# A fixed plan of scans per round, and row tiles loaded in the order in which the pairs change

## The chip, the cores and the metric

The kernel runs on one core of one Trainium2 chip. The metric is the device time of one execution in microseconds. Work on the core is done by TensorE (PE in the profile; PEld is its weight load), VectorE (DVE), ScalarE (ACT), GpSimd (POOL) and the DMA engines; SyncE (SP) issues most of the DMAs and computes nothing.

## What is computed

The input `x` has 2048 rows of 512 numbers, all float32. One half is softmax attention with 32 heads of 16 numbers each, the other a Fourier mixing of the same rows; a gate mixes the two.

```
g = sigmoid((x * gate_w).sum(-1, keepdims=True))
qkv = (x @ wqkv).reshape(B, S, 3, 32, 16)            # q, k, v
p = softmax(einsum("bhqd,bhkd->bhqk", q, k) * 16 ** -0.5, axis=-1)
a = einsum("bhqk,bhkd->bhqd", p, v).reshape(B, S, 512) @ wo
b = dft_seq_re @ (x @ dft_hid_re.T) - dft_seq_im @ (x @ dft_hid_im.T)
return g * a + (1 - g) * b
```

The weights are drawn large, so the softmax needs the row maximum taken off before the exponential.

## The kernel before

A **prologue** projects `x` to queries, keys and values, writes queries and keys to DRAM (`q_d`, `k_d`, each number as a high and a low part), and makes the operands of the Fourier half. Beside it run the first 320 **scans**. Then comes the **loop** `for m in range(MACROS)` of 256 rounds, and a short end.

The heads are handled in 16 **pairs** of two. For a pair two things are done, one after the other:

- **Scan** (`scan`, L624 and L626): the scores of a block of 128 queries against 512 keys are made on PE and reduced to their maximum by DVE (`mx<-s`). A pair takes 64 scans, each of two matmuls and two reductions (one for each head). When the last scan of a pair is done, `shift` (L179 to L182) turns the maxima into rows that are stored in `m_d`; its five parts stand in the list `late` and are given out among the tokens of the next two rounds.
- **Use** (`score`, L593 and L581; `pv`, L603): the scores are made again, transposed and with the maximum taken off inside the matmul, ACT takes their exponential, and PE multiplies by the values into the bank `pvb`. A pair takes 32 steps, that is 16 rounds; the first 8 rounds handle the first 1024 queries, the last 8 the others.

A **round** m holds two steps of use (8 scores and exponentials), some scans (before: 0 to 4), 6, 7 or 9 pairs of matmuls of the Fourier half and later of the output projection (`fill`, L840), and at its end the 16 value matmuls of the two steps before. The order of the matmuls in a round is written out by hand in a table `ORDERS`, by the numbers of scans and of fills; "c0 e1 s0" is a scan of head 0, a score of head 1, a fill of half 0.

Every 8 rounds (m = 8, 16, 24, ...) `pvb` is complete. `quotients` copies it on DVE (`ob`, L633), and POOL issues four small DMAs that gather the sums (`lc<-ob`, L636). At the head of round m + 2 DVE takes their reciprocal (`invert`, L643); it stands in DVE's queue ahead of all reductions of that round. POOL then spreads it and scales (rounds m + 4 and m + 6).

Scan and use of a pair each need its **row tiles** `qs` and `ks` (1.5 MB together) from DRAM, in two of six slots, so three pairs of tiles are held at a time: one in use, one being scanned, one loaded ahead. `load_scan` issues 8 DMAs on SP (L124); `load_use` issues the same 8 and then 6 small ones (ones, L138, and maxima from `m_d`, L140). SP takes its instructions in the order of the program; among them are the blocks of the Fourier matrices (`craw`, L208), stores (`y_d`, `bs_d`, `m_d`), and from time to time other loads. A slot falls free at the last matmul that reads it: for a pair in use at the end of a round 16p - 1, for a scanned one wherever its 64th scan stands.

Before, `prefetch(m)`, called at the head of each round, chooses what to load next when a slot pair is free: the next pair to scan or the next pair to use, by a guess of when the scan will end (`ends < 26`) and a rule that a pair to use is not loaded before the eighth step of the pair ahead. Scans are asked for at an even pace of 704/226 = 3.12 a round (`pace_`); a pair's first scan may be given only five rounds after its load (`scan_from`). Where the tiles are not there, a round gets fewer scans or none, and the next rounds get up to four until the plan is caught up with.

Of the kernel before, what the change touches and what calls it, by code (L numbers as in the profile page):

```python
# [23 lines left out]
NP = H // 2  # L24
# [7 lines left out]
PERIODS = 2 * NB  # L32
SCANS = 64
TOTAL = SCANS * NP
FRONT = 5 * SCANS
# [4 lines left out]
STEPS = NP * PERIODS  # L40
MACROS = STEPS // 2
OUTM = 234
SCAN_MACROS = 226
ENDS = {3: ("z0", "z1"), 8: ("z0", "z1"), 9: ("b3", "b4"), 10: ("b0", "b1"), 11: ("b2", "pv")}
ORDERS = {
# [12 lines left out]
def build(tc, x, xT, wqkv, wo, wrT, wiT, cr, ci, gate, out):  # L58
    nc = tc.nc
    with ExitStack() as ctx:  # L60
# [36 lines left out]
        def free_slots():  # L97
            return [i for i in range(6) if owner[i] is None]
# [10 lines left out]
        def release(who):  # L109
            for i in range(6):  # L110
                if owner[i] == who:
                    owner[i] = None

        def row_loads(p, queue, keys, who=None):

            qs, ks = (stacked([P, S], F32R, name, who) for name in ("qs", "ks"))
            loads = []
            for j in range(2):
                b, r = 64 * j, slice(DH * ((2 * p + j) % 8), DH * ((2 * p + j) % 8) + DH)
                loads += [(ks[b:b + 32, :], keys[p // 4][r, 0:1, :].to_broadcast([DH, 2, S])),  # L120
                          (qs[b:b + 32, :], q_d[p // 4][r, :, :].rearrange("e n s -> (e n) s")),
                          (ks[b + 32:b + 48, :], keys[p // 4][r, 1, :]),
                          (qs[b + 32:b + 48, :], q_d[p // 4][r, 0, :])]
            return (qs, ks), [lambda dst=dst, src=src: queue.dma_start(dst.bitcast(F32), src) for dst, src in loads]  # L124

        def load_scan(p, who=None):
            scanned[p], loads = row_loads(p, nc.sync, k_d, who)
            for load in loads:
                load()

        def load_use(p, who=None):
            used[p], loads = row_loads(p, nc.sync, k_d, who)
            for load in loads:
                load()
            qs, ks = used[p]
            for j in range(2):
                b = 64 * j + 48
                nc.sync.dma_start(ks[b:b + 2, :].bitcast(F32), ones_d)  # L138
                for n in range(2):
                    nc.sync.dma_start(qs[b + n:b + n + 1, :].bitcast(F32),  # L140
                                      m_d[p][n:n + 1, :, j].rearrange("n g b k -> n b g k"))
# [61 lines left out]
        def load_unit(pool, tag, bufs):  # L203
            if units:
                ph, t, u = units.pop(0)
                raw = pool.tile([P, D], F32, tag=tag, name="craw", bufs=bufs)
                raws_c.append(raw.rearrange("p (c q) -> p c q", q=P))
                nc.sync.dma_start(raws_c[-1], (cr, ci)[ph][t, :, u * CS:(u + 1) * CS, :])  # L208
# [12 lines left out]
        with ExitStack() as px:  # L221
# [101 lines left out]
            if True:  # L323
# [175 lines left out]
                def to_rhs(i):  # L499
                    def use(t, tx, ty):  # L500
                        ab = ep.tile([P, 512], F32, tag="eh", name="ab", bufs=3)
                        nc.gpsimd.tensor_add(ab, tx, ty)
                        after(7, nc.sync.dma_start, ab_d[i][t], ab)
                    return use
# [5 lines left out]
                use = to_rhs(1)  # L510
# [12 lines left out]
        with ExitStack() as pa:  # L523
# [23 lines left out]
            class Banks:  # L547

                slot, late, gap, load, group = 230.0, 434.0, 106.0, 200.0, 854.0
# [62 lines left out]
            scans, late = [FRONT, FRONT], []  # L612
# [93 lines left out]
            def output_rows(c):  # L706

                for f in range(ND - 1):
                    for i in range(2):
                        a = oc[c, f, i] = block((0, 18)[c % 2] + 2 * f + i)  # L710
                        src = o_d[f][i][c // 2, c % 2].rearrange("p (j r) s -> r (p j) s", j=2)
                        nc.sync.dma_start(a.bitcast(F32), src[0:DH])
# [10 lines left out]
            def load_y(c):  # L723
                y4 = stacked([P, 4, D], F32, "y4", ("y", c))
                nc.sync.dma_start(y4, y_d[c])
                for t in range(4 * c, 4 * c + 4):
                    ys[t] = y4[:, t % 4, :]
# [137 lines left out]
            def renew(s):  # L865
                ah[s], al[s] = block(2 * s), block(2 * s + 1)
                for i, v in enumerate((ah[s], al[s])):
                    nc.sync.dma_start(v.bitcast(F32), bs_d[s][i])
# [3 lines left out]
            def part_b(step):  # L872

                s, i = divmod(step, NB)
                for s, i in ((2 * s, i), (2 * s + 1, i - 4)):
                    if s < NB:
                        part_of_b(s, i)
# [22 lines left out]
            def order(nc_, ns):  # L900
                if (nc_, ns) in ORDERS:
                    return ORDERS[nc_, ns].split()
                base = ORDERS[(4, 7) if ns in (6, 7) else (0, 9)].split()
                for kind, have, want in (("c", 4 if ns < 9 else 0, nc_), ("s", 7 if ns < 9 else 9, ns)):
                    for j in range(2):
                        for _ in range(have - want):
                            base.remove(f"{kind}{j}")
                return base
# [3 lines left out]
            last = next_slot[0]  # L912
            for n, who in enumerate((("use", 0), ("use", 0), ("scan", FRONT // SCANS), ("scan", FRONT // SCANS))):
                owner[(last - 4 + n) % 6] = who
            use_loaded, scan_loaded = [0], [FRONT // SCANS]
            pace_ = (TOTAL - FRONT) / SCAN_MACROS
            scan_from = [0]

            def prefetch(m):

                p, i = divmod(2 * m, PERIODS)
                n = min(scans)
                while len(free_slots()) >= 2:
                    want_use = use_loaded[0] < NP - 1 and use_loaded[0] <= p and (
                        use_loaded[0] + 2) * SCANS <= n - 16 * bool(late)
                    want_scan = scan_loaded[0] < NP - 1 and scan_loaded[0] * SCANS <= n
                    ends = i + 2 * ((scan_loaded[0] + 1) * SCANS - n) / pace_
                    if want_scan and (not want_use or ends < 26):
                        scan_loaded[0] += 1
                        load_scan(scan_loaded[0], ("scan", scan_loaded[0]))  # L930
                        scan_from[0] = m + 5
                    elif want_use and i >= 8:
                        use_loaded[0] += 1
                        load_use(use_loaded[0], ("use", use_loaded[0]))
                    else:
                        return

            for m in range(MACROS):
                for step in (2 * m, 2 * m + 1):
                    part_b(step)  # L940
                for f in staged.pop(m, ()):
                    f()
                if m == 0:
                    for _ in range(2):
                        load_unit(ap, "craw", 2)
                if 2 * m % PERIODS == 0 and m:
                    release(("use", 2 * m // PERIODS - 1))
                prefetch(m)
                for ph, s in freed:
                    if ph == 0:  # L950
                        renew(s)
                    else:
                        if s == 2:
                            output_rows(0)
                        if s == 11:
                            output_rows(1)
                        if s in (5, 7, 9, 10, 11, 12):
                            next(operands, None)
                freed.clear()
                if m >= OUTM:  # L960
                    for _ in range(2):
                        next(operands, None)
                if m == OUTM - 2:
                    for c in range(2):
                        load_y(c)
                if 2 * m == (NP - 1) * PERIODS:
                    for c in (2, 3):
                        load_y(c)
                n = min(scans)
                want = min(TOTAL, FRONT + int(pace_ * (m + 1)))  # L970
                ready = min(TOTAL, (scan_loaded[0] + (m >= scan_from[0])) * SCANS)
                count_ = max(0, min(4, want - n, ready - n))
                for k, token in enumerate(order(count_, sizes[m])):
                    {"e": score, "c": scan, "s": fill}[token[0]](int(token[1]))
                    if late and k in (6, 13, 20):
                        late.pop(0)()
                for step in ((2 * m - 2, 2 * m - 1) if m else ()):
                    pv(step)
# [86 lines left out]
```

## Time and profile before

| | us |
|---|---|
| median of 3 runs | 1866.27 (1864.71 to 1867.63) |
| profiled execution, its own time | 1860.47 |
| its span | 1858.6 |
| PE busy | 1787.0 (96%) |
| DVE busy | 1334.2 (72%) |
| ACT busy | 1331.1 (72%) |
| POOL busy | 752.1 (40%) |

The profile shows one execution. The loop begins at about 365 us (the first score of L593) and ends near 1842 us (its last value matmuls); the rest is the prologue and the end. A round is seen most easily by its 16 value matmuls, which the view of the chain that ended last merges into one row, `PE pvb L603 x16`: the distance from one such row to the next is the length of a round. The columns of that view are the start in us, the length in us, and what ran.

### The profile page before, as it was taken

What the parts mean: (1) busy time and instruction counts of PE and PEld (TensorE: products, weight loads), DVE (VectorE), ACT (ScalarE), POOL (GpSimd) and SP (SyncE); (2) the same over time, 40 slices, a digit from 0 to 9 for tenths busy, and PEclk for the clock granted to TensorE, in tenths of its full rate; (3) what the DMA queues carried; (4) which work ended last, traced back from release to release, by engine and by line L of the source; (5) the groups of instructions that cost most, each with busy time, mean ns of one, the idle gap of its engine ahead of it and who ended that gap; (6) DMA issues with size and microseconds to landing.
All of it is one profiled execution on the core that took longest, in us unless ns stands there. A gap on an engine that the chain in (4) does not pass through costs nothing.

```text
span 1858.6 us, 36455 instructions
## 1 busy us (share of the span) xinstructions
PE 1787.0 (96%) x13640; PEld 1043.2 (56%) x13640; DVE 1334.2 (72%) x2367; ACT 1331.1 (72%) x2583; POOL 752.1 (40%) x878
## 2 busy tenths in 40 slices
PE   8998899899999999999999899999999899999998
PEld 7776677655555555555555455555554455555554
DVE  6797788777777774886877677668876676684334
ACT  5449898877777777666677677776676677767785
POOL 3685433544444455333333334343333344333122
PEclk9999999999999999999999999999999999999999
DMA  8673325653643444334245644342423343515522
GB/s 280 210 234 90 86 84 124 157 136 101 131 109 87 114 119 119 79 73 85 69 89 122 192 92 91 77 98 71 104 67 67 85 88 79 104 50 131 184 51 94
DMA packets 130529, 205.37 MB, mean 110 GB/s; under 512 B 54336, under 2 KB 56880, under 8 KB 123632
## 3 DMA queue, kind: packets, MB, share of 16 engines
q1 hardware_dynamic: 90000, 176.23, 36.8%
q0 software_dynamic: 38496, 19.47, 4.6%
q10 hardware_dynamic: 1856, 7.34, 1.5%
q8 instruction: 107, 1.75, 0.4%
q14 instruction: 70, 0.57, 0.1%
HBM read 136.71 MB, written 65.81 MB: 109 GB/s over the span
## 4 chain that ended last, share of the span: by engine, by line
PE 77%; DVE 6%; ACT 4%; POOL 4%; DMA 3%; issue 3%; DVEq 0%; ACTq 0%; POOLq 0%; SPq 0%
PE pvb L603 24%; PE z L840 20%; PE s L624 15%; PE s L593 13%; PE xy L189 3%; PE s L158 3%; DVE mx L626 3%; DMA lc<-ob 2%; ACT fold L162 2%; POOL el L245 1%; POOL s L245 1%; DVE ob L633 1%; ACT ty L407 1%; ACT tx L406 1%; DVE y L753 1%
## 5 line engine op out<-in xcount | busy, mean ns | idle before, releaser
L626 DVE TENSOR_REDUCE mx<-s 128x1 f32<-128x512 f32 x1408 | 919.1, 686 | 246.5 <-PE s L593 136.2
L581 ACT ACTIVATE e<-s 128x512 f32<-128x512 f32 x1082 | 607.9, 605 | 210.1 <-PE s L593 167.9
L581 ACT ACTIVATE eb<-s 128x512 f32<-128x512 f32 x966 | 550.4, 605 | 208.3 <-PE s L593 163.5
L593 PE MATMUL s<-qs,ks 50*128 50x512 f32 x2048 | 688.5, 420 | 0.7
L840 PE MATMUL z<-b,chi 64*128 64x512 f32 x2060 | 594.6, 405 | 0.0
L624 PE MATMUL s<-ks,qs 48*128 48x512 f32 x1408 | 529.2, 456 | 27.9 <-DVE mx L626 23.4
L603 PE MATMUL pvb<-e,va 128*17 128x512 f32 x2164 | 473.1, 595 | 0.0
L603 PE MATMUL pvb<-eb,va 128*17 128x512 f32 x1932 | 462.4, 595 | 0.0
L593 PEld LDWEIGHTS s<-qs,ks 50*128 50x128 f32 x2048 | 358.1, 187 | 95.0 <-ACT e L581 27.5
L624 PEld LDWEIGHTS s<-ks,qs 48*128 48x128 f32 x1408 | 215.0, 185 | 331.1 <-DVE mx L626 140.7
L840 PEld LDWEIGHTS z<-b,chi 64*128 64x128 f32 x2060 | 333.8, 187 | 22.3
L840 PE MATMUL z<-b,clo 64*128 64x512 f32 x1030 | 342.5, 404 | 0.0
L215 POOL CAST chi<-craw 128x512 fp32r<-128x512 f32 x126 | 77.3, 613 | 434.5 <-PE z L840 341.4
L164 DVE CUSTOM_DVE_ANT_0 fold<-s,fold 128x512 f32<-128x512 f32 x256 | 172.2, 690 | 49.4 <-ACT fold L162 38.3
L840 PEld LDWEIGHTS z<-b,clo 64*128 64x128 f32 x1030 | 177.5, 188 | 10.8
L216 POOL TENSOR_TENSOR clo<-craw,chi 128x512 fp32r<-128x512 f32 x126 | 161.4, 1281 | 44.1 <-PE z L840 32.4
L636 POOL DMA_DIRECT2D lc<-ob x124 | 63.3, 516 | 273.6 <-DVE ob L633 267.6
L162 ACT ACTIVATE fold<-s 128x512 f32<-128x512 f32 x256 | 146.8, 605 | 21.8 <-PE s L158 12.1
L158 PE MATMUL s<-ks,qs 48*128 48x512 f32 x512 | 135.3, 421 | 22.0 <-ACT fold L162 20.6
L603 PEld LDWEIGHTS pvb<-e,va 128*17 128x17 f32 x2164 | 84.5, 97 | 125.2 <-issue 125.2
L603 PEld LDWEIGHTS pvb<-eb,va 128*17 128x17 f32 x1932 | 81.3, 96 | 106.9 <-issue 106.9
L189 PE MATMUL xy<-w,b 64*128 64x512 f32 x768 | 130.4, 395 | 0.0
(121 smaller groups left out, 1562.7 us busy)
## 6 DMA issues: line engine op xcount, KB each, us to landing
craw<-cr SPq DMA_DIRECT2D x64, 256.0 KB
craw<-ci SPq DMA_DIRECT2D x64, 256.0 KB
ks<-k_d SPq DMA_DIRECT2D x56, 256.0 KB
qs<-q_d SPq DMA_DIRECT2D x56, 256.0 KB
ab_d<-ab SPq DMA_DIRECT2D x32, 256.0 KB
y_d<-y SPq DMA_DIRECT2D x32, 256.0 KB
b<-bs_d SPq DMA_DIRECT2D x32, 256.0 KB
ks<-k_d SPq DMA_DIRECT2D x56, 128.0 KB
```

Of the source, the lines that this page charges most:

```text
L158: nc.tensor.matmul(ps, qs[b:b + 48, qb * P:(qb + 1) * P], ks[b:b + 48, c * 512:(c + 1) * 512], start=True, stop=True)
L162: nc.scalar.activation(fold[j], ps, AF.Relu)
L164: nc.vector.tensor_tensor_reduce(out=fold[j], in0=ps, in1=fold[j], scale=1.0, scalar=-3.0e38, op0=ALU.add, op1=ALU.max, accum_out=mx[p][:, ...
L189: nc.tensor.matmul(ps[j], lhs[r], rhs[r], start=first, stop=last)
L215: copy(hi, raw)
L216: sub(lo, raw, hi.bitcast(F32))
L581: nc.scalar.activation(e, ps, AF.Exp, scale=SCALE)
L593: nc.tensor.matmul(ps, ks[b:b + 50, kb * P:(kb + 1) * P], qs[b:b + 50, q0:q0 + 512], start=True, stop=True)
L603: nc.tensor.matmul(pvb[r:r + VC, :], va[:, kb, 2 * p + j, :], es[step][c, j], start=kb == 0, stop=kb == NB - 1, tile_position=(0, r))
L624: nc.tensor.matmul(ps, qs[b:b + 48, qb * P:(qb + 1) * P], ks[b:b + 48, c * 512:(c + 1) * 512], start=True, stop=True)
L626: nc.vector.tensor_reduce(mx[p][:, j, qb, c:c + 1], ps, axis=AX.X, op=ALU.max)
L840: nc.tensor.matmul(ps, pr_.lhs(j), pr_.rhs(j), start=group.count[j] == 1, stop=group.count[j] == group.size)
```

## The change

The plan is fixed: three scans in each round, four in the first eight, until all 704 are given. The loads stand in one list, `changes`, sorted by the round in which the pair is first used or first scanned under that plan; whenever two slots are free, the next of the list is loaded, whatever its kind. The rule of the eighth step, the guess of the scan's end and the choice between the kinds are gone. A load for use still waits until its pair is scanned and its maxima are stored. Scans may begin two rounds after the load instead of five.

```diff
-SCAN_MACROS = 226
+EARLY = 8
...
-            use_loaded, scan_loaded = [0], [FRONT // SCANS]
-            pace_ = (TOTAL - FRONT) / SCAN_MACROS
+            scan_loaded = [FRONT // SCANS]
             scan_from = [0]
 
+            def planned(m):
+                return min(TOTAL, FRONT + 3 * (m + 1) + min(m + 1, EARLY))
+
+            changes = [(PERIODS // 2 * p, "use", p) for p in range(1, NP)]
+            for p in range(FRONT // SCANS + 1, NP):
+                changes.append((next(m for m in range(MACROS) if planned(m) >= p * SCANS), "scan", p))
+            changes.sort()
+
             def prefetch(m):
 
-                p, i = divmod(2 * m, PERIODS)
-                n = min(scans)
-                while len(free_slots()) >= 2:
-                    want_use = use_loaded[0] < NP - 1 and use_loaded[0] <= p and (
-                        use_loaded[0] + 2) * SCANS <= n - 16 * bool(late)
-                    want_scan = scan_loaded[0] < NP - 1 and scan_loaded[0] * SCANS <= n
-                    ends = i + 2 * ((scan_loaded[0] + 1) * SCANS - n) / pace_
-                    if want_scan and (not want_use or ends < 26):
-                        scan_loaded[0] += 1
-                        load_scan(scan_loaded[0], ("scan", scan_loaded[0]))
-                        scan_from[0] = m + 5
-                    elif want_use and i >= 8:
-                        use_loaded[0] += 1
-                        load_use(use_loaded[0], ("use", use_loaded[0]))
+                while changes and len(free_slots()) >= 2:
+                    _, kind, p = changes[0]
+                    if kind == "use":
+                        if (p + 1) * SCANS > min(scans) - 16 * bool(late):
+                            return
+                        load_use(p, ("use", p))
                     else:
-                        return
+                        load_scan(p, ("scan", p))
+                        scan_loaded[0], scan_from[0] = p, m + 2
+                    del changes[0]
...
-                want = min(TOTAL, FRONT + int(pace_ * (m + 1)))
+                want = planned(m)
```

Followed through by hand, round by round, the two rules give these rounds (the number of fills in a round does not change):

| scans and fills in a round | rounds before | rounds now |
|---|---|---|
| 3 scans, 7 fills | 82 | 125 |
| 3 scans, 6 fills | 48 | 99 |
| 4 scans, 7 fills | 42 | 7 |
| 4 scans, 6 fills | 35 | 1 |
| 2 scans, 6 or 7 fills | 3 | 0 |
| no scan, 7 fills | 7 | 0 |
| no scan, 6 fills | 20 | 5 |
| no scan, 9 fills | 19 | 19 |

Before, the rounds 62 to 66, 83, 84, 144 to 148 and 206 to 210 have no scan although some are left, and the scans end with round 226; now there is no such gap, and they end with round 231. The loads are given out in these rounds (u is a load for use, s one for scanning):

| | rounds of the loads |
|---|---|
| before | u4 s16 u21 s32 u42 u52 s62 u68 s80 u84 s96 u103 s112 u124 u132 s144 u148 s160 u165 s176 u185 u196 s206 u212 u230 |
| now | u0 s16 u19 s32 u40 s48 u62 u64 s80 u83 s96 u104 s112 u126 u128 s144 u147 s160 u168 s176 u190 u192 s208 u213 u235 |

Two places show what moves. The first is SP's queue at round 62. Before, a load for scanning (pair 8) stands there between two blocks of the Fourier matrices, and the maxima of pair 7 follow (`m_d_94`):

```order
L208 DMA craw<-cr 128x512
L124 DMA ks<-k_d_83 32x1x2048
L124 DMA qs<-q_d_79 32x2048
L124 DMA ks<-k_d_83 16x2048
L124 DMA qs<-q_d_79 16x2048
L124 DMA ks<-k_d_83 32x1x2048
L124 DMA qs<-q_d_79 32x2048
L124 DMA ks<-k_d_83 16x2048
L124 DMA qs<-q_d_79 16x2048
L208 DMA craw<-cr 128x512
L176 DMA m_d_94<-chi 128x32
L176 DMA m_d_94<-clo 128x32
```

Now the load for use of pair 4 (its end is shown: ones and maxima) and that of pair 5 stand almost behind one another, in rounds 62 and 64:

```order
L138 DMA ks<-ones_d 2x2048
L140 DMA qs<-m_d_91 1x64x32 x2
L138 DMA ks<-ones_d 2x2048
L140 DMA qs<-m_d_91 1x64x32 x2
L176 DMA m_d_94<-chi 128x32
L176 DMA m_d_94<-clo 128x32
L208 DMA craw<-cr 128x512
L124 DMA ks<-k_d_82 32x1x2048
L124 DMA qs<-q_d_78 32x2048
L124 DMA ks<-k_d_82 16x2048
L124 DMA qs<-q_d_78 16x2048
```

Pair 4's tiles are asked for two rounds before their first use, twelve rounds before it in the old order; one `craw` block is between the two loads.

The second place is DVE's queue around the quotient of round 64. Before, the copy of `pvb` and the reciprocal follow each other with no reduction between or just behind, since rounds 65 and 66 have no scan:

```order
L179 TENSOR_REDUCE m<-mx 128x32
L180 STREAM_TRANSPOSE mt<-m 128x32
L181 CAST chi<-mt 128x32
L182 TENSOR_TENSOR clo<-mt,chi 128x32
L751 TENSOR_SCALAR y<-z,gm 128x512
L753 SCALAR_TENSOR_TENSOR y<-z,gm,y 128x512
L633 COPY ob<-pvb 128x512
L643 RECIPROCAL lc<-lc 128x16
L626 TENSOR_REDUCE mx<-s 128x1 x46
```

Now the six reductions of round 65 stand between them, and those of round 66 and on behind the reciprocal:

```order
L182 TENSOR_TENSOR clo<-mt,chi 128x32
L626 TENSOR_REDUCE mx<-s 128x1 x14
L751 TENSOR_SCALAR y<-z,gm 128x512
L753 SCALAR_TENSOR_TENSOR y<-z,gm,y 128x512
L626 TENSOR_REDUCE mx<-s 128x1 x2
L633 COPY ob<-pvb 128x512
L626 TENSOR_REDUCE mx<-s 128x1 x6
L643 RECIPROCAL lc<-lc 128x16
L626 TENSOR_REDUCE mx<-s 128x1 x40
```

The same holds at every eighth round up to 224.

## The prediction

> **What bounds the kernel now.** I read the page first, then the chain of waits for the lengths of rounds, then the list of waits, and last the timelines of SP, POOL and DVE around the loads. From the page:
>
> ```profile
> PE 77%; DVE 6%; ACT 4%; POOL 4%; DMA 3%; issue 3%; DVEq 0%; ACTq 0%; POOLq 0%; SPq 0%
> lc<-ob POOLq DMA_DIRECT2D x124, 2.0 KB, 1.6
> ```
>
> PE holds three quarters of the chain, so the time is the sum of the rounds, and a round is what its matmuls and the bank hand-overs to ACT and DVE take. The chain of waits (start, length, what) gives the lengths: from one row of 16 value matmuls to the next.
>
> ```profile
> 737.14 1.84 PE pvb L603 x16
> 741.57 1.84 PE pvb L603 x16
> ...
> 754.02 1.84 PE pvb L603 x16
> 760.27 1.84 PE pvb L603 x16
> ...
> 830.25 1.89 PE pvb L603 x16
> 834.76 5.96 DMA lc<-ob
> 844.76 1.84 PE pvb L603 x16
> 849.47 1.84 PE pvb L603 x16
> ...
> 928.06 1.90 PE pvb L603 x16
> 939.43 1.84 PE pvb L603 x16
> ...
> 1018.54 1.89 PE pvb L603 x16
> 1023.04 8.30 DMA lc<-ob
> 1035.96 1.85 PE pvb L603 x16
> 1041.46 1.84 PE pvb L603 x16
> 1046.96 1.84 PE pvb L603 x16
> 1052.50 1.84 PE pvb L603 x16
> ...
> 1393.93 1.89 PE pvb L603 x16
> 1398.44 7.37 DMA lc<-ob
> 1410.41 2.17 PE pvb L603 x16
> ...
> 1444.56 1.88 PE pvb L603 x16
> 1449.06 8.36 DMA lc<-ob
> 1462.18 1.89 PE pvb L603 x16
> ```
>
> The reader is to see two things. First, lengths: a round of three scans takes 5.50 us (1035.96 to 1041.46, 6 fills) or 5.54 (1046.96 to 1052.50, 7 fills); one of four 6.25 (754.02 to 760.27, round 69); one of none 4.43 with 6 fills (737.14 to 741.57, round 66) and 4.71 with 7 (844.76 to 849.47, round 83). So the fourth scan costs 0.75 us, but a scan left out saves only a third of 1.07, 0.36. Second, the two rounds behind a quotient: 11.37 undisturbed (928.06 to 939.43, rounds 97 and 98), but 17.42 at 112, 16.48 at 176 and 17.62 at 184, with a wait for `lc<-ob` between: 6.05, 5.11 and 6.25 us lost. At 80 (four scans, so about 12.9) 14.51 is 1.6 lost. The list of waits (total, times, longest) has both ends of it:
>
> ```profile
> DVE lc L643 <- DMA lc<-ob: 44.8, 13, 6.0
> PE s L624 <- DVE mx L626: 23.4, 13, 4.9
> ```
>
> DVE stands at the reciprocal, the reductions behind it free no bank, and PE loses **23.4 us** in all at scan matmuls. Why `lc` is late the timelines show (start, length, queue):
>
> ```profile
> 825.17 0.33 SPq L755 DMA_DIRECT2D y_d<-y  x1
> 825.55 0.56 SPq L124 DMA_DIRECT2D ks<-k_d  x1
> 833.21 2.04 POOL L636 DMA_DIRECT2D lc<-ob  x4 [8.23 <-DVE ob L633]
> 840.84 0.25 DVE L643 RECIPROCAL lc<-lc 128x16 f32<-128x16 f32 x1 [2.86 <-DMA lc<-ob]
> 922.09 0.56 SPq L124 DMA_DIRECT2D ks<-k_d  x1
> 935.50 0.25 DVE L643 RECIPROCAL lc<-lc 128x16 f32<-128x16 f32 x1 [0.29 <-DMA lc<-ob]
> 1011.85 0.57 SPq L124 DMA_DIRECT2D ks<-k_d  x1
> 1031.53 0.25 DVE L643 RECIPROCAL lc<-lc 128x16 f32<-128x16 f32 x1 [5.97 <-DMA lc<-ob]
> 1387.88 0.56 SPq L124 DMA_DIRECT2D ks<-k_d  x1
> 1405.99 0.25 DVE L643 RECIPROCAL lc<-lc 128x16 f32<-128x16 f32 x1 [4.92 <-DMA lc<-ob]
> 1444.61 0.55 SPq L124 DMA_DIRECT2D ks<-k_d  x1
> 1457.54 0.25 DVE L643 RECIPROCAL lc<-lc 128x16 f32<-128x16 f32 x1 [5.77 <-DMA lc<-ob]
> ```
>
> `lc<-ob` lands in 1.6 us at the median, but at 80, issued until 835.25 behind a load of row tiles, it is there only at 840.84. From a load's first issue to the reciprocal it took 15.3 (80), 13.4 (96), 19.7 (112), 18.1 (176) and 12.9 us (184): the small DMAs come through when the 1.5 MB is nearly done. A quotient with no load beside it waits for nothing.
>
> **The change, part by part.** No matmul, reduction or DMA is added or removed; scans and loads move.
>
> *Rounds.* By the table of rounds: 43 more with three scans and 7 fills, +238.2 us; 51 more with 6, +280.5; 69 fewer with four, -431.3; 15 fewer without a scan and 6 fills, -66.5; 7 with 7 fills, -33.0; 3 with two scans (5.1, estimated between 4.43 and 5.50), -15.3. Sum **-27.4 us**. That is firm: each length comes from rounds of the same table of tokens. It counts the four scans of the first eight rounds (8 x 0.75). The scans' end in round 231 for 226 is in it too.
>
> *The loads at a quotient.* A load asked for in a round m that is a multiple of 8 is in flight when that round's `lc<-ob` is issued. Before, these were 16, 32, 80, 96, 112, 144, 160 and 176, and 185 just behind the quotient of 184: nine, and three of them harmless. Now they are the thirteen at 16, 32, and so on to 208, and also 40, 104 and 168: **sixteen**, each followed by rounds of three scans, where before some had the slack of a longer round (80, 160) or no reductions behind the reciprocal (144).
>
> How long may `lc` take? At 112 it came 19.7 us after the load and cost 6.05, so 13.65 were free; at 176 18.1 - 5.1 = 13.0. At 184 the load left with the value matmuls (1444.61 against 1444.56) and 12.9 - 6.25 = 6.7 were free; the load of 96 left 5.97 ahead of them (922.09, 928.06), so that is 12.7 on the same footing. Mean **13.1** for a load that leaves that early, that is when its slot falls free. The value matmuls begin 5.54 - 1.84 = 3.7 after the start of a round, so early means 2.3 ahead of it. A load that leaves at the round's start, as at 80 right behind a `y_d` store, has **10.8**. Arrivals: 13.4 at best, 19.7 at worst; where no load was seen at that place I take 14.8, between the quiet 96 and the crowded 176 and nearer to the first, as at 80.
>
> - Early (32, 96, 112, 144, 176, 208): 32 and 96 at 13.4, 0.3 each; 112 and 176 as before, 6.05 and 5.1; 144 and 208 14.8 - 13.1 = 1.7 each. Sum 15.2. 48 leaves about 1 us later: 2.7.
> - At the round's start (16, 80, 160; and 40, 104, 168, whose slot falls free with the last scan of the round before): 6 x (14.8 - 10.8) = 24.
> - Behind another load (64, 128, 192), next.
>
> *Loads for use two rounds ahead of their use.* Pairs 4, 8 and 12 are asked for in 62, 126 and 190 and first used in 64, 128 and 192. A load for use in the trace:
>
> ```profile
> 1128.97 0.56 SPq L124 DMA_DIRECT2D ks<-k_d  x1
> 1141.69 2.01 SPq L140 DMA_DIRECT2D qs<-m_d  x2
> ```
>
> Its last DMA has been issued 14.7 us after the first; SP waits in between until the rows have landed. Two rounds are 11.0. So the first scores of the pair wait 2 to 4 us, and SP, which takes its queue in order, gets to the next load (64, 128, 192) some 2.4 us after the round's plain start. `lc` then has 10.8 - 2.4 = 8.4 us: 6.4 lost by round 66, with the first wait in it, as that moves the due time by as much. With fewer blocks right behind the rows I take 6 each: 18.
>
> Together 15.2 + 2.7 + 24 + 18 = **60 us** of waits in place of 23.4. Net -27.4 + 60 - 23.4 = **+9 us**. The profiled execution takes 1860.47 (span 1858.6), 5.8 under the median; the sum makes it 1869.7, and the median 1866.27 becomes **1875**.
>
> Taken as nothing: scanning two rounds after the load (16, 80, 144, 208), since only the last scan of round m + 2 reads the new tile, some 14 us after the issue, and the rows precede `lc`, whose wait is counted; without that cover it would be 1 to 3 us each. The load for use of pair 1 in round 0 and that of pair 15 in 235, beside 2 MB of `y` loads, have 16 and 5 rounds to land. SP is held for 10 to 15 us by each; the `craw` blocks behind it are loaded two blocks of 1.7 rounds ahead (19 us), which covers it.
>
> A rule speaks for another outcome. The Trainium skill, page "DMA: Bandwidth & Descriptors", section "Queues, rings and completion order", says that each DMA engine serves the queues it has work for in turn, a packet at a time. By it `lc<-ob`, on POOL's queue, would pass between the packets of SP's load and the waits would be near nothing. This trace disagrees (5.6 us behind the last issue at 80).
>
> **The rivals.**
>
> 1. *The waits stay small; faster.* Place: `lc<-ob` behind the sixteen loads. If each arrives after 13.4, as at 96, the losses are 0.3 x 6 + 1.3 + 6 x 2.6 + 3 x 5 = 34, and the time 27.4 + 23.4 - 34 = 17 us under before: **1849**. It decides from a mean loss of 3.2 us per load down (50.8 / 16). For it: 96, and 184 at 12.9. Against it: 80, 112 and 176 have not done so, and the even rounds leave less time than rounds of four scans.
> 2. *SP becomes the bound in 62 to 66, 126 to 130, 190 to 194.* Two loads for use hold SP for some 27 us, with one `craw` block between them, where the fills take a block every 9.5 us and have 19 in hand. If blocks run out, up to 8 us at each of the three, +24: **1899**. Against it: a block needs to be split only one block ahead of its use, which gives some more.
> 3. *`lc` passes the load*: its small DMAs come through between those of the row tiles, and all waits go: 1866.3 - 27.4 - 23.4 = **1815**. Against it stand the rows of 80, 112 and 176. This is what the skill's rule would make of the change.
> 4. *The plan is not kept*: a tile is not loaded when its scans are due, and rounds without scans and with four come back. Then about as before, **1866**. The order of the changed program has six reductions in each round there; I find no gap.
>
> **How the numbers follow.** The forecast has 0.58 (losses of 48 to 72, 1863 to 1887), rival 1 0.22, rival 2 0.15, rival 3 0.03, rival 4 0.02. Arrivals of 13.4 and of about 16.5 for all give 1849 and about 1900; leaving out 2 in 10 the range is 1852 to 1896. The forecast's own is 1863 to 1887. A change under 0.2% (3.7 us) cannot be told from none: the low end of the forecast (0.11) and rival 4 make that 0.13; rivals 1 and 3 make faster 0.25; the rest, 0.62, is slower.
>
> **What would show it.** Right: no round without a scan before 232, and 5.50 or 5.54 us in the undisturbed rounds; `DVE lc L643 <- DMA lc<-ob` near 90 us in all and PE's wait on `mx` doubled; long rounds at 18, 42, 50, 66, 82, 106, 114, 130, 162, 170, 178 and 194, and a wait of scores for `m_d` at the start of 64, 128 and 192. Wrong: `lc` there within 11 us of most loads; the three-scan rounds themselves longer or shorter, which makes the -27.4 false; waits of `chi` for `craw` on POOL and of fills behind it, which is rival 2.

## The result, and the profile after

| kernel | median, us | lowest to highest | runs | ratio to before (95%) |
|---|---|---|---|---|
| before | 1864.22 | 1860.68 to 1868.41 | 10 | |
| with the change | 1865.54 | 1860.00 to 1871.10 | 10 | 1.0006 (0.9990 to 1.0021) |

No difference can be measured. The forecast of 1875 was 9.5 us too high; the range held the time, and the outcome had been given 0.13. The profiled execution of the changed kernel took 1871.10 us (span 1869.3), the longest of its ten, while that of before (1860.47) lies at the low end of its own. Two single profiles would therefore tell a difference of 10.6 us that the medians do not have, and losses are taken below from three profiles of each kernel.

The page of the changed kernel, the chain that ended last, by engine and by line:

```profile
PE 74%; DMA 8%; ACT 4%; DVE 4%; issue 3%; POOL 3%; SPq 1%; DVEq 0%; ACTq 0%; POOLq 0%
PE pvb L603 22%; PE z L840 18%; PE s L624 14%; PE s L593 12%; PE xy L189 5%; DMA lc<-ob 4%; DMA qs<-q_d 3%; PE s L158 3%; ACT fold L162 2%; DVE mx L626 1%; DVE ob L633 1%; SPq L124 1%; POOL lc L636 1%; ACT ty L407 1%; POOL el L245 1%
```

DMA has gone from 3% of the chain to 8%. Two names carry it: `lc<-ob`, the wait that was there before, and `qs<-q_d`, the row tiles themselves. The list of waits of the changed kernel (total, times, longest) has both:

```profile
DVE lc L643 <- DMA lc<-ob: 46.6, 17, 6.8
PE s L624 <- DVE mx L626: 32.7, 16, 5.7
PE s L593 <- DMA qs<-m_d: 8.4, 2, 5.4
PE s L593 <- DMA m_d<-clo: 3.8, 1, 3.8
```

PE now stands for 32.7 us at scan matmuls, where it was 23.4, and 12.2 us in three waits of scores at the start of 64, 128 and 192, which did not exist before. In the chain of waits of the changed kernel (start, length, what), first round 48, whose load leaves early enough (652.98 in SP's timeline, 5.9 us ahead of its value matmuls), then round 112:

```profile
658.87 1.89 PE pvb L603 x16
...
670.11 1.84 PE pvb L603 x16
675.64 1.85 PE pvb L603 x16
...
1016.45 1.84 PE pvb L603 x16
1021.95 1.84 PE pvb L603 x16
1027.45 1.89 PE pvb L603 x16
...
1031.95 9.11 DMA lc<-ob
...
1045.89 1.90 PE pvb L603 x16
```

The undisturbed rounds take 5.50 (1016.45 to 1021.95, 1021.95 to 1027.45) and 5.53 us (670.11 to 675.64), as the rounds of three scans did before. Two rounds behind a quotient take 11.24 when `lc` is there in time (658.87 to 670.11) and 18.44 at 112 (1027.45 to 1045.89): 7.2 lost. The same chain at round 64:

```profile
725.75 1.84 PE pvb L603 x16
...
735.28 10.42 DMA qs<-q_d
...
745.78 2.75 DMA m_d<-clo
...
759.26 1.84 PE pvb L603 x16
```

The last rows of the load for use of pair 4 (issued by SP at 735.28, L124) land 10.4 us later, SP then issues what reads and writes `m_d`, and only then do the scores begin.

Where the losses lie, in us over the usual length of a round of the same kind, worked out from the ends of all 256 groups of value matmuls; the mean of three profiles of each kernel:

| place | predicted | before | now |
|---|---|---|---|
| behind loads that leave early (32, 48, 96, 112, 144, 176, 208) | 17.9 | | 15.1 |
| behind loads at the round's start (16, 40, 80, 104, 160, 168) | 24 | | 21.8 |
| loads for use at 64, 128, 192, and the quotients there | 18 | | 21.8 |
| behind all loads, before (16 to 184) | 23.4 | 25.3 | |
| round 5 | 0 | 0 | 4.3 |
| round 235 | 0 | 6.0 | 0.9, in 237 |
| others above 0.35 | | 3.3 | 1.3 |
| all | | 34.6 | 65.2 |

The loop got 27.2 us shorter by its plan (the usual lengths of all 256 rounds sum to 1432.7 before and 1405.5 now) and lost 30.6 more. The two nearly cancel: from the start of round 2 to the end of round 255 it takes 1460.5, 1461.8 and 1465.0 us before, and 1470.2, 1463.5 and 1465.9 now, which is 4.1 more in the mean of three, 1.3 in the medians of ten runs.

### The profile page after: what moved, and what is told of

The parts are those of the page before. It is cut to its first block, busy times and chain, and to the rows that moved or that the text cites. A ratio compares the mean times of both kernels' runs of the same rounds, so it can differ in the third digit from the quotient of the medians.

```text
span 1869.3 us, 36447 instructions
## 1 busy us (share of the span) xinstructions
PE 1778.0 (95%) x13640; PEld 1020.0 (55%) x13640; DVE 1337.5 (72%) x2367; ACT 1330.6 (71%) x2583; POOL 752.4 (40%) x878
## 4 chain that ended last, share of the span: by engine, by line
PE 74%; DMA 8%; ACT 4%; DVE 4%; issue 3%; POOL 3%; SPq 1%; DVEq 0%; ACTq 0%; POOLq 0%
PE pvb L603 22%; PE z L840 18%; PE s L624 14%; PE s L593 12%; PE xy L189 5%; DMA lc<-ob 4%; DMA qs<-q_d 3%; PE s L158 3%; ACT fold L162 2%; DVE mx L626 1%; DVE ob L633 1%; SPq L124 1%; POOL lc L636 1%; ACT ty L407 1%; POOL el L245 1%
## 5 line engine op out<-in xcount | busy, mean ns | idle before, releaser
L581 ACT ACTIVATE e<-s 128x512 f32<-128x512 f32 x1082 | 597.0, 603 | 236.7 <-PE s L593 171.4
L581 ACT ACTIVATE eb<-s 128x512 f32<-128x512 f32 x966 | 537.3, 603 | 192.5 <-PE s L593 119.4
L624 PE MATMUL s<-ks,qs 48*128 48x512 f32 x1408 | 512.0, 467 | 35.6 <-DVE mx L626 32.7
L603 PE MATMUL pvb<-e,va 128*17 128x512 f32 x2164 | 461.7, 597 | 0.0
L603 PE MATMUL pvb<-eb,va 128*17 128x512 f32 x1932 | 447.8, 600 | 0.0
L593 PEld LDWEIGHTS s<-qs,ks 50*128 50x128 f32 x2048 | 366.9, 189 | 83.2 <-issue 13.1
L624 PEld LDWEIGHTS s<-ks,qs 48*128 48x128 f32 x1408 | 208.0, 188 | 373.9 <-DVE mx L626 169.7
L840 PEld LDWEIGHTS z<-b,chi 64*128 64x128 f32 x2060 | 348.6, 191 | 24.3 <-POOL chi L215 2.3
L840 PE MATMUL z<-b,clo 64*128 64x512 f32 x1030 | 333.4, 405 | 0.2 <-POOL clo L216 0.2
L158 PE MATMUL s<-ks,qs 48*128 48x512 f32 x512 | 135.3, 421 | 22.9 <-ACT fold L162 21.5
```

Source lines behind the costliest of these rows:

```text
L158: nc.tensor.matmul(ps, qs[b:b + 48, qb * P:(qb + 1) * P], ks[b:b + 48, c * 512:(c + 1) * 512], start=True, stop=True)
L581: nc.scalar.activation(e, ps, AF.Exp, scale=SCALE)
L593: nc.tensor.matmul(ps, ks[b:b + 50, kb * P:(kb + 1) * P], qs[b:b + 50, q0:q0 + 512], start=True, stop=True)
L603: nc.tensor.matmul(pvb[r:r + VC, :], va[:, kb, 2 * p + j, :], es[step][c, j], start=kb == 0, stop=kb == NB - 1, tile_position=(0, r))
L624: nc.tensor.matmul(ps, qs[b:b + 48, qb * P:(qb + 1) * P], ks[b:b + 48, c * 512:(c + 1) * 512], start=True, stop=True)
L840: nc.tensor.matmul(ps, pr_.lhs(j), pr_.rhs(j), start=group.count[j] == 1, stop=group.count[j] == group.size)
```

## The experiments

Four questions were open: whether the profiled executions stand for the kernels; whether the wait for `lc` is what takes the gain; why `lc` is late; and where the 6 us at the end of the loop in before come from, which the prediction did not have.

### The two kernels again

Both kernels unchanged, once with twelve timed runs each and once more with a single, profiled run.

> The kernel before, unchanged, for a second profile. Theory A (the sum was right for one execution, but the profiled one before was a quick one): the long rounds at 18, 82, 114, 162, 178 and 186 lose 26 to 34 us here, 23.5 in the first profile. Theory B (executions hardly differ; the first profile is typical): 21 to 26 us. Time ratio to before 1.000 within 0.002 by both.

> The changed kernel, unchanged, for a second profile. Its first profile was the slowest of ten runs: the long rounds lost some 67 us against the medians of their kind. Theory A: this profile loses 50 to 62 us, and the difference to before comes from arrivals that change from run to run. Theory B: 64 to 70 us again. Ratio 1.000 to 1.002.

> The changed kernel unchanged, a third profile. Theory A: rounds 2 to 255 lose 60 to 70 us against the usual length of their kind (68.9 and 62.1 in the first two), of which 5, 64, 128 and 192 some 22.

> The kernel before unchanged, a third profile. Theory A: 32 to 36 us lost (32.5 and 34.1 in the first two), 5 or so of it in round 235.

Before: 1863.74 (12 runs, 0.9997, 0.9982 to 1.0012), and 1866.65 in the single run. With the change: 1864.63 (12 runs, 1.0006, 0.9986 to 1.0026), and 1868.2 in the single run. The losses above 0.35 us sum to 32.5, 34.1 and 37.1 in the three profiles of before and to 68.9, 62.1 and 64.6 in those of the changed kernel. So the profile from which the prediction was made was the one with the least losses, and the one of the changed kernel that with the most. The repeats do not decide between the two theories: the six long rounds lost 25.9 us in the second profile of before, at the border of both ranges, and 62.1 in the second of the changed kernel lies between them. That the change makes no difference stands on 22 runs of it.

### The reciprocal one round later

The quotient's three steps are given to rounds m, m + 3, m + 5, m + 7 instead of m, m + 2, m + 4, m + 6 (the last pair as it was). `lc` then has one round more to arrive, and nothing else moves. In the changed kernel and in the one before, the same line:

```
-  for n, f in zip((2, 4, 6) if p < NP - 1 else (2, 3, 4), divide(*quotients(p, h))):
+  for n, f in zip((3, 5, 7) if p < NP - 1 else (2, 3, 4), divide(*quotients(p, h))):
```

> The changed kernel with the reciprocal, the spread and the scaling one round later (rounds m + 3, m + 5, m + 7). Theory L (DVE standing at the reciprocal ahead of the reductions is what costs PE the time): the losses at 18, 42, 82, 106, 114, 162, 170, 178 and 194, some 43 us, fall to under 6, since lc was at most 6.2 us late and gets 5.5 more; the first waits at 64, 128 and 192 (18 us) and at 5 (4 us) stay; time 0.976 to 0.982 of before. Rival S (the row tiles' traffic slows the rounds anyway, and the reciprocal only shows it): under 10 us saved, 0.995 to 1.001.

> The kernel before with the same later reciprocal. Theory L: its 23 to 30 us of long rounds go, 0.984 to 0.988. Together with e3 this gives the worth of the plan alone: after_late under before_late by 27 (rounds) less 22 (waits for late row tiles at 5, 64, 128 and 192), that is by 3 to 10 us. Rival S: 0.997 to 1.000.

In the changed kernel: 1834.33 (1829.59 to 1843.32, 6 runs), 0.9844 (0.9817 to 0.9872). In the kernel before: 1843.24 (1840.88 to 1845.80, 6 runs), 0.9888 (0.9865 to 0.9911). The waits of the changed kernel with the later reciprocal:

```profile
PE s L593 <- DMA qs<-m_d: 14.3, 3, 5.5
PE s L624 <- DMA qs<-q_d: 6.4, 3, 3.3
PE s L624 <- DVE mx L626: 3.9, 5, 2.6
DVE lc L643 <- DMA lc<-ob: 2.5, 5, 0.9
```

DVE's wait for `lc` falls from 46.6 to 2.5 us and PE's wait behind it from 32.7 to 3.9; the losses at 42, 106, 114, 162, 170, 178 and 194 are gone. So the wait for `lc` is the cause of these, and it was worth about 30 us in the changed kernel and 20 in the one before. With it away, 8.9 us lie between the two. They are not the plan's shorter rounds alone: in round 235 the kernel before, where the load of 230 still stands, now loses 10.0 us (PE stands 6.9 us for DVE's `y` at L785), the changed kernel 1.6.

The gain of the changed kernel is less than was expected, and the list says why. A new wait stands in it: scans waiting for row tiles, `PE s L624 <- DMA qs<-q_d`, three times, 6.4 us. It had been there all the time, hidden behind the wait for `lc`: rounds 18 and 82 still lose 5.8 and 3.2. And 64, 128 and 192 lose 7.0, 8.1 and 6.9, since no reciprocal is involved there.

### The rest of the losses, one part each

Each on top of the later reciprocal. The losses are read from one profile each: that of the later reciprocal alone was the longest of its six runs (1843.32), that of the nine early rounds the shortest of its own (1823.04). The times with the later reciprocal, in both kernels, and those of the four kernels below all lie above the top of what was expected, by 0.06 to 0.24% of the time before.

The loads for use of pairs 4, 8 and 12 one round sooner, three rounds ahead of their use and not two, by a ninth round of four scans:

```
-EARLY = 8
+EARLY = 9
```

> e3 (the changed kernel with the later reciprocal) with four scans in the first nine rounds instead of eight, so that pairs 4, 8 and 12 are loaded for use three rounds ahead of their use, not two. Theory U (the scores at 64, 128 and 192 wait for late row tiles, 22 us in e3): two thirds or more of it goes, less 1 to 6 us for scan tiles that are read a third of a round earlier at 18, 82, 146 and 210: 0.976 to 0.981 of before. Rival (these rounds are long because SP or the DMA engines are full, whenever the load starts): 0.984 as e3.

1830.72 (1823.04 to 1834.25, 6 runs), 0.9830 (0.9801 to 0.9859). Rounds 64 and 192 lose nothing now and 128 loses 1.2, where they lost 22.0 together; but its waits also show

```profile
PE s L624 <- DMA qs<-q_d: 9.9, 4, 3.6
```

so the scans' wait for their tiles has grown from 6.4 to 9.9 us, at 18, 82, 146 and 210 (4.9, 5.4, 2.1 and 1.5 lost). The intervals of the two kernels overlap; it is the trace that shows the loads for use as the cause of 64, 128 and 192, not the time.

The load for use of pair 1 not in round 0, between the `y` loads, but from round 4 on:

```
-  if (p + 1) * SCANS > min(scans) - 16 * bool(late):
+  if m < 4 or (p + 1) * SCANS > min(scans) - 16 * bool(late):
```

> e3 with the load for use of pair 1 in round 4, as before the change, not in round 0. Theory: the long round 5 (3.9 us in the changed kernel, 1.2 in e3) goes, nothing else: 0.982 to 0.984. Rival: it costs as much in round 8 or later, 0.984 to 0.986.

1835.65 (1829.86 to 1838.56, 6 runs), 0.9851 (0.9823 to 0.9880). Round 5 loses 0.3 us here. But it loses 0.3 also in the kernel with nine early rounds and in the next one, where this load stands in round 0 as before, and 1.2 with the later reciprocal alone. So the run does not show that the load's place costs the 4.3 us there, and the time is not told apart from the kernel without this edit.

Scans of a new pair three rounds behind its load, not two:

```
-  scan_loaded[0], scan_from[0] = p, m + 2
+  scan_loaded[0], scan_from[0] = p, m + 3
```

> e3 with scans beginning three rounds after the load instead of two. Theory T (at 18 and 82 the last scan waits for its row tile, which the late reciprocal hid in the changed kernel; 10 us in e3 with 146 and 210): these four rounds come down to 5.1 us or so, and the next have four scans and 6.25: 6 to 9 us less than e3, 0.979 to 0.982. Rival (another tile or bank is waited for there): 0.984 or more.

1830.83 (1828.85 to 1835.60, 6 runs), 0.9832 (0.9806 to 0.9858). Nothing is lost at 18, 82, 146 and 210; left are 6.3, 6.8 and 6.7 at 64, 128 and 192 and 3.1 at 235. So the tile that is scanned two rounds after its load is late once `lc` does not hide it.

All four edits together:

> All four: later reciprocal, nine early rounds, pair 1 in round 4, scans three rounds after their load. If the losses are what the theories say, and they add up: the rounds of the plan and nearly nothing else, 1862.7 - 27 (rounds) - 24 (reciprocal) = 1812 to 1818, 0.973 to 0.976. If each gives back elsewhere: 0.980 or more.

1818.80 (1816.98 to 1822.18, 6 runs), 0.9766 (0.9741 to 0.9792): 43.6 us under the kernel before, and the fastest of all. Its chain at round 112:

```profile
1006.35 1.89 PE pvb L603 x16
1009.31 1.33 POOL lc L636 x3
1010.85 9.47 DMA lc<-ob
...
1020.51 0.25 DVE lc L643
1023.79 1.84 PE pvb L603 x16
```

`lc` takes as long as ever (9.47 us against 9.11), but the chain passes a reciprocal that has a round more, and the three rounds from 1006.35 to 1023.79 take 17.44, only 0.7 over the 16.74 that 11.24 and another 5.50 would make. All its losses, small ones too, sum to 21.0 us, those of the kernel before with the later reciprocal to 21.0 as well; the usual lengths of their rounds sum to 1408.5 and 1432.7, a difference of 24.2, and the medians (1818.80 and 1843.24) differ by 24.4. That the two sums of losses are equal is chance: 10.0 of the kernel before stand in round 235, and 2.3 of this one. So the rounds do get shorter by the plan's sum, but the agreement to 0.2 us is luck.

### Whose queue holds `lc`

The prediction saw that `lc<-ob` comes when the row tiles are nearly through, not why. It is issued by POOL; here ACT issues it, whose DMAs go by another queue.

```
-  nc.gpsimd.dma_start(lc[32 * n:32 * n + 32, :],
+  nc.scalar.dma_start(lc[32 * n:32 * n + 32, :],
```

> The changed kernel with the gathers lc<-ob issued by ACT's queue instead of POOL's. ACT then waits for the copy ob at each quotient, some 1 us, 31 times. Theory F (lc waits until the row tiles in front of it are through, whoever issues it): lc again lands 12 to 19 us after the load's first issue, the long rounds stay, time 1.00 to 1.02 of before. Rival Q (it is late because of POOL's own queue; the DMA engines would serve another queue in turn): lc lands within 2 to 3 us of its issue, the long rounds at 42, 82, 106, 114, 162, 170, 178 and 194 go (some 30 us), time 0.985 to 1.00.

2014.74 (2012.64 to 2019.95, 4 runs), 1.0807 (1.0773 to 1.0841). The timeline of rounds 80 and 112 (start, length, queue or engine, idle before):

```profile
874.12 0.56 SPq L124 DMA_DIRECT2D ks<-k_d  x1
880.24 0.69 DVE L633 COPY ob<-pvb 128x512 f32<-128x512 f32 x1 [0.66 <-PE pvb L603]
880.96 2.63 ACTq L636 DMA_DIRECT2D lc<-ob  x4
...
1073.46 0.57 SPq L124 DMA_DIRECT2D ks<-k_d  x1
1081.67 0.69 DVE L633 COPY ob<-pvb 128x512 f32<-128x512 f32 x1 [1.01 <-PE s L593]
...
1093.73 2.44 ACTq L636 DMA_DIRECT2D lc<-ob  x4
1096.21 0.60 ACT L581 ACTIVATE eb<-s 128x512 f32<-128x512 f32 x1 [15.96 <-DMA lc<-ob]
```

The issue takes place on ACT itself: 2.6 us in which no exponential is made, and at 112, beside a load, ACT can issue only at 1093.73 although `ob` is done at 1082.36, so that it stands for 15.96 us. Every round behind a quotient became 2.7 to 17 us longer, also those without a load, some 4 us each. So ACT was far dearer than expected, and the time says nothing about queues. The packets do: at 80 the four DMAs have been issued by 883.59, the row tiles end at 886.97, and the packets of `lc` are moved between 886.19 and 887.70. At 160 the four have been issued by 1402.69, the row tiles end at 1404.69, and the packets of `lc` are moved between 1405.08 and 1405.67. At 88, with no load, they are issued until 932.84 and the last packet ends at 933.65. On ACT's queue `lc` comes when the rows are through, as on POOL's. It is not POOL's queue that holds it; whether it is the DMA engines' backlog of 1.5 MB or what feeds them was not taken apart further.

### The end of the loop before

In the kernel before, with pair 15's load for use in round 235, where the change puts it, instead of 230:

```
-  want_use = use_loaded[0] < NP - 1 and use_loaded[0] <= p and (
+  want_use = use_loaded[0] < NP - (2 if m < 235 else 1) and use_loaded[0] <= p and (
```

> The kernel before with the load for use of pair 15 in round 235, where the changed kernel has it, instead of 230. Theory E (round 235 loses 5 to 6 us because lc, the y tiles and the load of 230 crowd there; the change takes this load away): round 235 under 2 us over its usual 5.07, and 0.997 to 0.998 of before. Rival (another part of the change did it): 235 stays at 5 or more lost, 1.000.

1856.45 (1852.19 to 1861.76, 10 runs), 0.9962 (0.9947 to 0.9977): 6.6 us less than the 13 runs of the kernel before beside it (1863.05). The chain of waits of the kernel before, from the value matmuls of round 232 to those of 235:

```profile
1718.44 1.84 PE pvb L603 x16
...
1724.29 7.09 DMA y_d<-y
...
1739.19 1.84 PE pvb L603 x16
```

The timelines of SP, DVE and PE there (start, length, queue or engine, idle before):

```profile
1700.62 0.57 SPq L124 DMA_DIRECT2D ks<-k_d  x1
...
1713.34 2.41 SPq L140 DMA_DIRECT2D qs<-m_d  x2
1715.79 0.59 SPq L761 DMA_DIRECT2D y<-y_d  x1
...
1729.74 0.25 DVE L643 RECIPROCAL lc<-lc 128x16 f32<-128x16 f32 x1 [5.49 <-DMA lc<-ob]
...
1731.61 0.48 DVE L687 MEMSET wor<- 128x512 f32 x1 [1.07 <-DMA y_d<-y]
...
1733.55 0.80 PE L840 MATMUL z<-b,b 64*128 64x512 f32 x2 [3.35 <-DVE y L785]
```

and the chain of the kernel with the load five rounds later, from 232 on:

```profile
1719.87 1.86 PE pvb L603 x16
...
1729.39 1.84 PE pvb L603 x16
```

In the first the three rounds take 20.75 us (1718.44 to 1739.19), in the second the first two take 9.52 and nothing waits for a `y` DMA. The load in 230 keeps SP from 1700.62 to 1715.75, the load of `y` behind it goes out at 1715.79, in the other kernel at 1702.51; and the store `y_d<-y`, issued soon after, takes 7.09 us, for which DVE waits, and PE behind it. DVE stands there first for `lc` (5.49 us, until 1729.74) and only the last 1.07 us for the store; with the later reciprocal, where `lc` is not in the way, the store alone keeps it for 10.03 us in the kernel before. That the load's place costs these 6 us is shown by the run; that it does so through SP's queue is read from the rows.

## Why the prediction was right in part, and wrong in the sum

- **Rounds, -27.4.** Right. The usual lengths sum to 27.2 less, and the fastest kernel against the one before with the later reciprocal has its 24.2 in the medians (that they agree to 0.2 us is luck, as said above).
- **Sixteen loads at a quotient, 60 in place of 23.4.** Right in mechanism and nearly in size: 58.7 in the same three classes. Within them the sums came out (15.1, 21.8, 21.8 against 17.9, 24, 18), the single places did not: 50 and 66 lost nothing, 130 only 0.8 in one of three profiles, and 64, 128 and 192 lost 4.7 to 8.0 in their own round. Before, the losses behind loads were 25.3 in the mean of three profiles, not 23.4. The later reciprocal shows the mechanism: it takes DVE's wait for `lc` from 46.6 to 2.5 us.
- **Pair 15 in 235, taken as nothing.** This is the step that failed. The prediction asked whether the load would be late at its new place, and it is not. It did not ask what the load did at its old place: in 230 it held SP in front of the last `y` loads and cost the kernel before 6.0 us in round 235. Moving that load alone gave 6.6 us. The row was in the trace of before, as a wait of 3.4 us of PE for DVE's `y` at L785, and was not read, because the sum was made only over the waits that the change was expected to add to.
- **Pair 1 in round 0, taken as nothing.** Wrong the other way: 4.3 us in round 5. By the rows the load itself has time, but SP stands for it, and behind it in SP's queue is `braw`, for which POOL stands, and behind that in POOL's order the `chi` of the fills. In the changed kernel's chain (start, length, what):

```profile
381.17 11.28 DMA qs<-q_d
394.61 4.93 DMA braw<-ab_d
...
401.56 0.61 POOL chi L215
```

  No run shows it: with the later reciprocal and the load still in round 0, round 5 lost 1.2 us in one kernel and 0.3 in two, and 0.3 also with `lc` on ACT's queue. Why it lost 3.9 to 4.9 in all three profiles of the changed kernel stays open.

- **Scanning two rounds behind the load, covered by `lc`; without that cover 1 to 3 us each.** The cover was there, and without it the price was 5.8 at 18, 3.2 at 82, 1.0 at 146 and 0.6 at 210.
- **What would show it.** A `DVE lc` wait near 90 us was wrong: 46.6. With six reductions between the copy of `pvb` and the reciprocal, DVE comes later to its wait and stands there less; before, part of its 44.8 fell into rounds with nothing to reduce and cost nothing (3.57, 3.87 and 4.39 behind the quotients of 64, 144 and 208). DVE's own wait was the wrong row to foretell from; PE's rows were right.
- **The rivals.** Waits that stay small: they did not. SP as the bound in 62 to 66 and its like: the fills did not starve there; it happened in round 5 instead. The plan not kept: it was kept, round by round. `lc` passing the load: refuted by the waits at 112 and 162, and on ACT's queue again. The Trainium skill, page "DMA: Bandwidth & Descriptors", section "Queues, rings and completion order", says that each DMA engine serves its queues in turn, a packet at a time, which would make the passing likely. The rows disagree (9.11 us to the landing at 112).

With the sizes as measured the sum becomes -27.2 + 63.0 (the waits with round 5) - 25.3 - 5.1 (round 235 less 237) = +5.4 instead of +9.2; with the small losses elsewhere (1.3 now, 3.3 before) it is +3.4. The loops of three profiles give +4.1, and the six profiled executions themselves differ by 3.9 in the mean (1867.3 less 1863.3). The medians of ten runs give +1.3; the 2 to 3 us between lie within what executions of one kernel differ by, and stay open. The last 2 us of the miss are the starting point: 1866.27 was the median of three runs, 1864.22 that of ten.

## What to carry to other kernels

Before a piece of work is moved, price the place that it leaves as carefully as the one that it goes to: a load in an ordered queue costs whatever stands behind it there. Here DVE's reciprocal, waiting for a DMA, held up all the reductions behind it; so place such an instruction by the slowest arrival and not by the usual one. One round of delay for a result that nobody needed sooner was worth 30 us. And when a wait is removed, look for the second one that it hid.

## What the runs showed of the hardware

**A wait of PE can cost more than its length, since the clock may go down behind it.** PE's timeline at the waits of round 112 and of 162, with the idle time before, and the same wait of 162 in the second profile of the changed kernel; first the one kernel:

```profile
1042.11 0.79 PE L624 MATMUL s<-ks,qs 48*128 48x512 f32 x1 [5.67 <-DVE mx L626]
1322.66 0.79 PE L624 MATMUL s<-ks,qs 48*128 48x512 f32 x1 [3.07 <-DVE mx L626]
```

its busy time in the stretches behind (length, PE busy, granted clock, DMA share, GB/s):

```profile
1042.00:1046.00 4.00, 3.89 (x20) 0.50 0.86 304
1322.00:1326.00 4.00, 3.34 (x16) 0.57 0.05 7
```

and then both views of the second profile, PE's timeline

```profile
1316.91 0.50 PE L624 MATMUL s<-ks,qs 48*128 48x512 f32 x1 [1.76 <-DVE mx L626]
```

and the stretch behind:

```profile
1316.00:1320.00 4.00, 3.09 (x24) 1.00 0.02 4
```

After 5.67 and 3.07 us of idling the granted clock is 0.50 (the 0.57 has the idle end of the wait in it), and 16 to 20 matmuls run where 24 do after 1.76 us at full clock. Round 162 lost 4.4 us in the one execution and 1.9 in the other. The length of the wait alone does not decide it. Between 380 and 1842 us, in the fourteen profiles of all kernels here, the 8 waits of PE from 0.9 to 1.4 us left the clock at 1.00, and the 59 of 2.79 us and more brought it to between 0.50 and 0.78 in the 3 us behind them. Of the 57 between 1.4 and 2.79 us 35 lowered it and 22 did not. Two of these, from the third profile of before (round 162) and from the changed kernel with the later reciprocal (round 82), with a stretch behind each:

```profile
1313.81 0.50 PE L624 MATMUL s<-ks,qs 48*128 48x512 f32 x1 [1.41 <-DVE mx L626]
1315.00:1316.00 1.00, 1.00 (x8) 0.50 0.00 0
853.84 0.47 PE L624 MATMUL s<-ks,qs 48*128 48x512 f32 x1 [2.76 <-DMA qs<-q_d]
855.00:856.00 1.00, 1.00 (x12) 1.00 0.92 86
```

The Trainium skill, page "TensorE: Matmul & The Clock Gate", section "HAM oscillation — how this bites in real kernels", gives gaps of more than about 3.4 us as those to avoid. Here 1.41 were enough once.

It is no small part of the result. Worked out in stretches of 1 us from 380 to 1740, the time at a lowered clock, each stretch counted with what is missing to 1.00 (so at most this much is lost):

```
before                         10.2  13.4  11.5
with the change                27.3  22.2  25.6
with the change, later lc      13.7
before, later lc                5.1
all four edits                  1.7
```

About 13 (25.0 in the mean less 11.7) of the 30.6 us that the changed kernel loses more than the one before can be this. That can be why PE's waits in the list (32.7 and 12.2) make only two thirds of the 68.9 us that the rounds of that execution lost. The prediction had it without knowing: its losses were lengths of rounds, so the slow matmuls behind a wait were in them.

**A load of 1.5 MB took 10.7 to 17 us in the loop of the changed kernel, from its first issue to the end of its last 8 KB packet, and the small DMAs of `lc` end with it.** At 112 of the changed kernel it was issued from 1021.57, its last 8 KB packet ended at 1038.64, and the last of `lc` at 1040.01; without a load `lc` lands about 1 us after its last issue.
